# LSH attention and a token-mixing layer on one core: a new order of the same work, from a planner with other durations

## The chip, the cores and the metric

The kernel runs on one core of a Trainium2 chip. A time is the device time of one execution in microseconds (us). The kernel before was run three times; beside these there is one execution under the hardware profiler, with its own time and its trace.

The engines are named as in the profile: PE is TensorE (matmul), PEld its weight loads, DVE is VectorE, ACT is ScalarE, POOL is GpSimd, and SP is the queue from which all DMA is issued here.

## The reference

Four batches of eight heads, 768 positions, head size 64. Queries and keys are hashed to six sign bits by a random projection, a query sees only the keys of its own bucket, and the attention output, put together to 4 x 768 x 512, goes through a layer that mixes tokens with a phase:

```python
q_bits = (np.einsum('bhsd,dk->bhsk', q, proj) > 0)          # k alike; bits -> bucket
mask = q_bucket[:, :, :, None] == k_bucket[:, :, None, :]
scores = np.where(mask, scale * np.matmul(q, k.transpose(0, 1, 3, 2)), -1e9)
attn = np.exp(scores - np.max(scores, axis=-1, keepdims=True))
attn = attn / (np.sum(attn, axis=-1, keepdims=True) + 1e-09)
x = concat_heads(np.matmul(attn, v))                        # 4 x 768 x 512
theta = x @ w_theta
y = einsum('ts,bsd->btd', w_tok_r, x * np.cos(theta)) + einsum('ts,bsd->btd', w_tok_i, x * np.sin(theta))
u = x + y
out = u + np.maximum(u @ w_ch, 0.0)
```

## The kernel before

**Attention.** The unit is a *step*: one pair of heads, 128 rows of queries, all 768 keys; four batches of four pairs of six row tiles make 96 steps. In a trace or an order a step is written batch_pair_row, so 2_1_5 is the last row tile of the second pair of the third batch. A step runs through all engines:

- PE writes the scores of both heads, tile `st` (16 matmuls, two heads side by side). The bucket test is inside, as a rank-12 term of `rows` and `kb` with a large factor. Both halves of the PSUM pool "s" are taken by one step, so the scores of the next step start only as the exponentials of this one are done.
- DVE takes the maximum of each row of `st` (`mc`, L709) and makes shift and factor of it (L712, L715); ACT makes the exponential `pf` (L719), once for each head.
- ACT rounds `pf` to float16 (`pp`, L725), and POOL makes the rest as a second float16 (L731).
- SP issues a DMA transpose of both parts (`pt<-pp`, L735), one for each head.
- PE multiplies with the values (`po`, 18 matmuls for each head), which loads `pt` as weights. After three row tiles DVE divides (L767 to L779) and writes `x`.

`pb` are the matmuls of the hash bits, once for a pair of heads. Queries, keys, values and weights are split into a high and a low part on ACT, DVE and POOL.

**The layer.** When a batch's `x` is complete, PE transposes it (`pt_x`), multiplies with w_theta (`ps_th`, three matmuls in each part), ACT and DVE make cosine and sine (`z`, L895 and L896, which need another activation table than the exponential), PE multiplies over tokens (`py`, 36 matmuls for each of six row tiles), transposes (`pt_u`) and multiplies with w_ch (`ps_r`). The layer of one batch is put between the attention steps of the next; that of the last batch stands behind all attention.

**What sets the order.** Nothing is ordered by hand. The code builds a list of operations, each with a priority, one or more engines with a duration in ns, the operations it waits for and the buffers it takes (`op(...)`). `issue_all` plays that list through a model of the five engines: whenever an engine of the model is free, it takes the ready operation with the lowest priority number, and the instruction is emitted there. The order on each engine's queue is the order of these decisions; the chip then works each queue off in that order. The priority of an attention operation is its step number g plus an offset (`VM`, `PF`, `KA`, `KB`, `KT`, `KV`, `KN`); weights, values, queries and the layer have offsets of their own (`W0`, `WS`, `QK0`, `QK1`, `TH0`, `Y0`, `YS` and so on, those with `_0` and `_3` for the first and the last batch). `wl`, `wmul`, `qkl`, `sign`, `zl`, `zh` and `mag` name two engines, and the one that is free first gets them. Where PE in the model has nothing ready in the first 190 us of the model's time, a matmul on constants is emitted (`fill`), which keeps the clock up and computes nothing. Three tables bear on PE:

```python
AFTER = {"pv": 94, "vall": 70, "y": 17}
WIDE = {"st", "proj", "bits"}
if best is not None and o.name in WIDE:     # L241: another ready operation came first
if e != "PE" or o.name not in WIDE or AFTER.get(before, 0) < 50:   # L245
```

`pv` is `po` of the trace, `y` is `py`, `proj` is `ps_th` and `ps_r`, `bits` is `pb`. An operation in `WIDE` that would stand right behind a `pv` is put off for another ready one of about the same priority.

Of the kernel before, what the change touches and what calls it, by code (L numbers as in the profile page):

```python
# [31 lines left out]
def lsh_attention_moe_kernel(ctx: ExitStack, tc: tile.TileContext, qk, wt, v, consts, w_theta, w_ch, out):  # L32
# [59 lines left out]
    LAZY = dict.fromkeys(("wlow", "whigh", "wsign", "wabs", "wscale", "wmul", "wth", "wtl", "wh", "wl"), 200)  # L92
    WAKE = {"ACT": 45, "DVE": 37, "PE": 58, "POOL": 105, "SP": 40}
    AFTER = {"pv": 94, "vall": 70, "y": 17}
    WIDE = {"st", "proj", "bits"}
    SHARED = {"qkl", "p1", "p2", "zf", "zh", "zl", "mag", "wlow", "whigh", "wmul", "wl", "vv2", "wtl"}

    class Slot:
# [21 lines left out]
    def op(name, prio, alts, deps=(), slots=(), table=None):  # L120
        return Op(name, prio, alts, deps, slots, table)
# [472 lines left out]
    def prep_qk(b, hp, G, g):  # L594
        t = {}
# [34 lines left out]
        for lo, n_ in ((0, 512), (512, S - 512)):  # L630
            def signs(lo=lo, n_=n_):
                sm_ = Slot("m")
                u = {}

                def bits():
                    u["pb"] = bank(sm_, [P, 512], f"pb_{b}_{hp}_{lo}")
                    cols = slice(lo, lo + n_)
                    mm(u["pb"][:, :n_], pst["q"], t["hl"][:, 0, 0, cols], True, False)
                    mm(u["pb"][:, :n_], pst["k"], t["hl"][:, 0, 1, cols], False, False)
                    mm(u["pb"][:64, :n_], pst["q"][:, :64], t["hl"][:, 1, 0, cols], False, False)  # L640
                    mm(u["pb"][:64, :n_], pst["k"][:, :64], t["hl"][:, 1, 1, cols], False, True)

                def total():
                    if "sum" not in t:
                        t["rows"], t["kb"] = rowt[sr.idx], kbt[sr.idx]
                        t["sum"] = ap_.tile([56, S], F32, tag=sq.tag, bufs=1, name=f"sum_{b}_{hp}")
                    u["s"] = t["sum"][:, lo : lo + n_]
                    ACT.activation(u["s"], u["pb"][64:120, :n_], AF.Copy)

                def plus():  # L650
                    DVE.tensor_tensor(u["s"], u["pb"][:56, :n_], u["s"], ALU.subtract)

                def sign(eng):
                    return lambda: eng.tensor_scalar(t["rows"][:56, lo : lo + n_], u["s"], affs[:56, 0:1], affs[:56, 1:2], ALU.is_ge, ALU.mult)

                pr1 = G + at("QK1", b) + early
                b1 = op("bits", pr1, on("PE", 10 + 925 * n_ / 512, bits), hs + ls + [proj_ready], [sm_, sh])
                b1 = op("btot", pr1, on("ACT", 75 + 425 * n_ / 512, total), [b1], [sm_, sq, sr])
                b1 = op("bplus", pr1, on("DVE", 70 + 540 * n_ / 512, plus), [b1], [sm_, sq])
                fs.append(op("sign", pr1, {"DVE": (190 + 270 * n_ / 512, sign(DVE)), "POOL": (230 + 1940 * n_ / 512, sign(POOL))}, [b1], [sq, sr]))  # L660

            signs()
# [14 lines left out]
    def step(g, b, hp, i, t, vt, po):  # L677
# [15 lines left out]
                        l, r = (t["rows"][rows, ts(i, P)], t["kb"][rows, k0:k1]) if a == 2 else (hl[rows, a, 0, ts(i, P)], hl[rows, c, 1, k0:k1])  # L693
                        mm(st[j][:, k0:k1], l, r, n == 0, n == 3)

        a = op("st", g, on("PE", 1450, scores), t["ready"], ss + t["slots"])
        for j in range(2):
            def head(j=j):
                nonlocal a
# [47 lines left out]

                gj = g + DJ * j
                m = op("vmax", gj + VM, on("DVE", 865, vmax), [a], [ss[j], smc])
                m = op("factor", gj + VM, on("DVE", 70, factor), [m], [smc])  # L750
                m = op("shift", gj + VM, on("DVE", 70, shift), [m], [smc])
                e = op("pf", gj + PF, on("ACT", 680, pf), [m], [ss[j], smc, spf], table="exp")
                k1 = op("p1", gj + KA, pick(g, P1, {"ACT": (700, p1("ACT")), "DVE": (470, p1("DVE"))}), [e], [spf, spp])
                k2 = op("p2", gj + KB, pick(g, P2, {"DVE": (870, p2(DVE)), "POOL": (1650, p2(POOL))}), [k1], [spf, spp])
                d = op("turn", gj + KT, on("SP", [(1550, 515000)], turn), [k2], [spp, spt])
                po["done"] = op("pv", gj + KV, on("PE", 560, pv), [d] + po["wait"], [spt, po["slot"], vt["slot"], sx])
                po["wait"] = [po["done"]]

# [19 lines left out]
                rc = po["rc"].rearrange("p (i j) -> p i j", j=2)[:, :, j]  # L778
                DVE.scalar_tensor_tensor(dst, po["acc"][:, :, j, :D], vt["inv"], rc.unsqueeze(2).to_broadcast([P, HT, D]), ALU.mult, ALU.mult)  # L779

        r = op("total", g + KN, on("DVE", 90, total), [po["done"]], [po["slot"]])
        r = op("recip", g + KN, on("DVE", 70, recip), [r], [po["slot"]])
        n = op("norm", g + KN, on("DVE", 2 * 340, norm), [r], [po["slot"], sx])
        for k in range(lo, i + 1):
            xready[b][k].append(n)

# [184 lines left out]
    g = 0  # L971
# [19 lines left out]
BUFS = {'hl': 2, 'rows': 2, 'sum': 1, 'mc': 3, 'pf': 3, 'pp': 4, 'pt': 4, 'vb': 1, 'tmp': 3}  # L991
TAIL = ["m", "s"]
WIN = {"m": 3, "tmp": 3, "s": 2}
PF = -0.541
KA = 1.061
KB = 1.686
KT = 28.046
KV = 1.273
KN = 2.14
DJ = 0.23  # L1000
VM = -1.125
AB = -1.13
WTH = 23.785
WTS = -0.332
WC = 27.23
WCS = 0.768
P1 = [[0, 999, ['ACT']]]
P2 = [[0, 999, ['POOL']]]
GR = 2
GR1 = 0  # L1010
GROUPS = [[(0, 3), (3, 6)], [(0, 4), (4, 6)], [(0, 2), (2, 4), (4, 6)]]
TH0_3 = 1.836
TH1_3 = 0.0
Y0_3 = 15.352
YS_3 = 9.104
Y1_3 = 0.075
PV0_0 = -2.213
QK0_0 = -2.499
QK1_0 = -17.278
HOLD = 0.575  # L1020
FILL = 190000
TH0_0 = 0.433
TH1_0 = 0.727
Y0_0 = 12.725
Y1_0 = 2.214
YS_0 = 6.989
PEN = 1.489
AHEAD = 1.866
H0 = -9.299
PST = 19.565  # L1030
QKL = -13.487
QK0 = -4.416
QK1 = -4.289
PV0 = -2.541
LV0 = 1.74
W0 = 7.559
WS = 4.063
TH0 = 1.218
TH1 = 0.164
Y0 = 9.384  # L1040
YS = 6.051
Y1 = 2.833

EXTRA_INT = {"BUFS": [dict(hl=2, rows=2, sum=1, mc=3, pf=a, pp=b_, pt=c, vb=1, tmp=3) for a, b_, c in ((2, 3, 3), (3, 4, 4), (2, 4, 5), (3, 5, 3), (3, 3, 5), (2, 5, 4))]}
EXTRA_TUNE = ["DJ", "VM", "KT"]
# [51 lines left out]
```

## Time and profile before

| | |
|---|---|
| median of three runs | 810.58 us (808.44 to 811.03) |
| the profiled execution | 813.75 us, its span in the trace 811.9 us |
| PE busy | 771.1 us (95% of the span), 113.0 us of it filler |
| DVE, ACT, POOL busy | 564.8, 537.9 and 471.2 us (70, 66 and 58%) |
| matmuls | 7218, of which 463 are filler |
| DMA | 117.30 MB, 192 transposes |

The span is 1.85 us shorter than the time of the same execution, and that execution is 3.2 us (0.4%) above the median of the three others. The profile has for each group of instructions the busy time, the mean of one and the idle time just before it with its releaser. The busy time of PE is no measure of work done, since a matmul's end is modelled and follows its start by more than the next one needs; what one costs in a row of equal ones is the distance of their starts.

### The profile page before, as it was taken

The numbers are of one execution on the slowest core, as the hardware profiler recorded it, in microseconds if no ns is written. First come the engines' busy times: TensorE is split into PE (matmuls) and PEld (weight loads), VectorE is DVE, ScalarE is ACT, GpSimd is POOL, SyncE is SP. The second block draws the span as 40 slices with busy tenths as digits, with TensorE's granted clock in tenths as the row PEclk, the third lists the DMA queues.
The fourth block names the chain that finished last, engine by engine and source line by source line (L and its number), as shares of the span: only waits on it lengthen the run. The fifth ranks groups of instructions, "written<-read, shape, count | busy, mean of one in ns | idle before, by whom it ended". The sixth has DMA issues, their size and how long they took to land. (4 is left out here: it accounts for less than half of the span.)

```text
span 811.9 us, 18205 instructions
## 1 busy us (share of the span) xinstructions
PE 771.1 (95%) x7218; PEld 511.7 (63%) x7218; DVE 564.8 (70%) x1207; ACT 537.9 (66%) x712; POOL 471.2 (58%) x331
## 2 busy tenths in 40 slices
PE   9999998999997999999989999999999999999998
PEld 4556565667764466676756666667756776675456
DVE  6777887888878766676896566776876755557323
ACT  5767786677987675666996666666986665548101
POOL 4657665766765785756657576665476565533300
PEclk9999999999999999999999999999999999999999
DMA  6899999996575788978637998997339888850002
GB/s 221 181 184 214 168 230 226 172 213 137 89 161 115 152 169 155 191 160 170 111 73 146 161 180 158 185 182 165 59 74 191 158 132 156 148 113 0 1 1 78
DMA packets 322916, 117.30 MB, mean 144 GB/s; under 512 B 307920, under 2 KB 312016, under 8 KB 322832
## 3 DMA queue, kind: packets, MB, share of 16 engines
q1 hardware_dynamic: 322832, 116.15, 72.4%
q8 instruction: 56, 0.92, 0.5%
q14 instruction: 28, 0.23, 0.1%
HBM read 32.54 MB, written 6.29 MB: 48 GB/s over the span
## 5 line engine op out<-in xcount | busy, mean ns | idle before, releaser
L731 POOL TENSOR_TENSOR pp<-pf,pp 128x768 f16<-128x768 f32 x192 | 325.0, 1713 | 190.8 <-ACT pp L725 179.8
L719 ACT ACTIVATE pf<-st,mc 128x768 f32<-128x768 f32 x192 | 180.9, 988 | 119.1 <-DVE mc L715 73.7
L709 DVE TENSOR_REDUCE mc<-st 128x1 f32<-128x768 f32 x192 | 175.1, 950 | 84.0 <-PE st L83 83.6
L83 PE MATMUL py<-z,wtk 128*128 128x512 f16 x864 | 202.0, 379 | 1.0 <-DVE z L873 1.0
L83 PE MATMUL st<-hl 64*128 64x512 f32 (+1 forms) x1152 | 159.5, 355 | 7.2 <-ACT pf L719 6.7
L83 PEld LDWEIGHTS <-pt 128*128 128x128 f16 x3456 | 122.5, 98 | 54.8 <-DMA pt<-pp 27.3
L83 PE MATMUL po<-vv,pt 128*128 128x65 f16 (+1 forms) x3456 | 138.2, 195 | 16.9 <-DMA pt<-pp 14.8
L725 ACT ACTIVATE pp<-pf 128x768 f16<-128x768 f32 x192 | 152.7, 839 | 0.2
L83 PEld LDWEIGHTS st<-hl 64*128 64x128 f32 x1152 | 111.2, 186 | 57.3 <-ACT pf L719 29.2
L83 PEld LDWEIGHTS <-wtk 128*128 128x128 f16 x864 | 78.4, 98 | 85.5 <-issue 4.0
L83 PE MATMUL fill<-idle 128*128 128x512 f16 x463 | 113.0, 389 | 1.8 <-DVE ones L75 1.5
L918 POOL TENSOR_TENSOR z<-f,z 128x512 f16<-128x512 f32 x37 | 49.7, 1358 | 59.9 <-ACT z L912 40.6
L83 PE MATMUL st<-kb,rows 64*128 64x256 f32 (+1 forms) x384 | 81.0, 337 | 0.0
L83 PEld LDWEIGHTS <-idle 128*128 128x128 f16 x463 | 42.8, 100 | 49.4 <-issue 5.2
L83 PE MATMUL ps_r<-wch,h_u 128*128 128x512 f32 x192 | 64.8, 419 | 0.0
L83 PE MATMUL ps_th<-wth,h_x 128*128 128x512 f32 x192 | 62.7, 407 | 1.8 <-DVE l_x L838 1.4
L907 DVE SCALAR_TENSOR_TENSOR f<-x,zr,z 128x512 f32<-128x512 f32 x48 | 52.7, 1122 | 7.8 <-ACT z L895 5.1
L834 ACT ACTIVATE h_u<-pt_u 128x512 fp32r<-128x512 f32 x24 | 14.2, 594 | 58.1 <-PE pt_u L829 53.8
L83 PEld LDWEIGHTS st<-kb,rows 64*128 64x128 f32 x384 | 50.5, 187 | 3.2
L83 PE MATMUL ps_r<-wch,l_u 128*128 128x512 f32 x96 | 38.6, 402 | 3.3 <-DVE l_u L838 3.3
L83 PEld LDWEIGHTS ps_th<-wth,h_x 128*128 128x128 f32 x192 | 34.2, 189 | 10.2 <-DVE l_x L838 2.1
L83 PE MATMUL ps_th<-wth,l_x 128*128 128x512 f32 x96 | 38.2, 398 | 0.7 <-DVE l_x L838 0.7
(110 smaller groups left out, 875.6 us busy)
## 6 DMA issues: line engine op xcount, KB each, us to landing
nat<-in_qk_dram SPq DMA_DIRECT2D x32, 384.0 KB
wst<-in_wt_dram SPq DMA_DIRECT2D x12, 768.0 KB
vb<-in_v_dram SPq DMA_DIRECT2D x16, 384.0 KB
out_dram<-x SPq DMA_DIRECT2D x24, 256.0 KB
pt<-pp SPq DMA_TRANSPOSE x192
w_th<-in_moe_w_theta_dram SPq DMA_DIRECT2D x4, 512.0 KB
w_ch<-in_moe_w_ch_dram SPq DMA_DIRECT2D x8, 256.0 KB
kb<-rows SPq DMA_DIRECT2D x32, 36.0 KB
```

The lines of the kernel that those rows point to most:

```text
L83: PE.matmul(out_, l, r, start=start, stop=stop, skip_group_check=True)
L709: DVE.tensor_reduce(col(0), st[j], AX.X, ALU.max, negate=True)
L719: ACT.activation(u["pf"], st[j], AF.Exp, bias=col(2), scale=col(1))
L725: ACT.activation(u["pp"][:, 0], u["pf"], AF.Copy)
L731: return lambda: eng.tensor_tensor(u["pp"][:, 1], u["pf"], u["pp"][:, 0], ALU.subtract)
L834: ACT.activation(u["hi"], u["pt"], AF.Copy)
L907: DVE.scalar_tensor_tensor(u["f"], tl[b][:, tt], t["zr"][:, 2 * tt + r : 2 * tt + r + 1], t["zw"][r][:, tt], ALU.mult, ALU.mult)
L918: return lambda: eng.tensor_tensor(t["z"][r, 1][:, tt], u["f"], t["z"][r, 0][:, tt], ALU.subtract)
```

## The change

No instruction of the computation is added or taken away, no buffer count changes, and no size. What changes are the numbers from which the planner works: durations, the table `WIDE`, and all the offsets. The diff, with two lines for the table of offsets:

```diff
-    WIDE = {"st", "proj", "bits"}
+    WIDE = {"proj", "bits"}
...
-                b1 = op("bits", pr1, on("PE", 10 + 925 * n_ / 512, bits), hs + ls + [proj_ready], [sm_, sh])
+                b1 = op("bits", pr1, on("PE", -80 + 1080 * n_ / 512, bits), hs + ls + [proj_ready], [sm_, sh])
...
-        a = op("st", g, on("PE", 1450, scores), t["ready"], ss + t["slots"])
+        a = op("st", g, on("PE", 1600, scores), t["ready"], ss + t["slots"])
...
-                m = op("factor", gj + VM, on("DVE", 70, factor), [m], [smc])
-                m = op("shift", gj + VM, on("DVE", 70, shift), [m], [smc])
-                e = op("pf", gj + PF, on("ACT", 680, pf), [m], [ss[j], smc, spf], table="exp")
-                k1 = op("p1", gj + KA, pick(g, P1, {"ACT": (700, p1("ACT")), "DVE": (470, p1("DVE"))}), [e], [spf, spp])
-                k2 = op("p2", gj + KB, pick(g, P2, {"DVE": (870, p2(DVE)), "POOL": (1650, p2(POOL))}), [k1], [spf, spp])
-                d = op("turn", gj + KT, on("SP", [(1550, 515000)], turn), [k2], [spp, spt])
+                m = op("factor", gj + VM, on("DVE", 63, factor), [m], [smc])
+                m = op("shift", gj + VM, on("DVE", 121, shift), [m], [smc])
+                e = op("pf", gj + PF, on("ACT", 875, pf), [m], [ss[j], smc, spf], table="exp")
+                k1 = op("p1", gj + KA, pick(g, P1, {"ACT": (733, p1("ACT")), "DVE": (470, p1("DVE"))}), [e], [spf, spp])
+                k2 = op("p2", gj + KB, pick(g, P2, {"DVE": (870, p2(DVE)), "POOL": (1610, p2(POOL))}), [k1], [spf, spp])
+                d = op("turn", gj + KT, on("SP", [(1475, 720000)], turn), [k2], [spp, spt])
...
-        n = op("norm", g + KN, on("DVE", 2 * 340, norm), [r], [po["slot"], sx])
+        n = op("norm", g + KN, on("DVE", 655, norm), [r], [po["slot"], sx])
...
-KT = 28.046
-KV = 1.273
+KT = 55.822
+KV = 1.387
...
-W0 = 7.559
-WS = 4.063
+W0 = 27.21
+WS = 20.711
```

The second number of `turn` is a size from which the model works out how long a transpose holds the DMA engines: 515000 / 360 = 1430 ns before, 720000 / 360 = 2000 ns now.

What comes out is the same work in another order on every queue: 454 filler matmuls instead of 463; one more change to the sine table and back (in the layer of the third batch); and some operations that may run on two engines go to the other one, of which the most are six `zl` (L918) from POOL to DVE and three products of the token weights (L489, L490) from DVE to POOL. Three places follow.

PE, third batch, between the scores of step 2_1_5 and those of 2_2_0; `pt0` and `pt1` are the transposed exponentials of the two heads, and a row of `po` stands for 18. Before:

```order
L83 LDWEIGHTS pt0_2_1_3_6752
L83 MATMUL po_2_1_3_6825<-vv_2_1_5707,pt0_2_1_3_6752 128x65
...
L83 LDWEIGHTS pt1_2_1_3_6776
L83 MATMUL po_2_1_3_6825<-vv_2_1_5707,pt1_2_1_3_6776 128x65
...
L83 MATMUL ps_r1_1_6871<-wch0_3604,h_u1_1_6724 128x512
...
L83 MATMUL st0_2_2_0_6900<-hl_2_2_6243 128x512
```

and now:

```order
L83 LDWEIGHTS pt0_2_1_3_6739
L83 MATMUL po_2_1_3_6818<-vv_2_1_6176,pt0_2_1_3_6739 128x65
...
L83 MATMUL py_1_3_6574<-z1_1_5253,wtk0_95 128x512
...
L83 MATMUL ps_r1_1_6849<-wch0_3384,h_u1_1_6716 128x512
...
L83 LDWEIGHTS pt1_2_1_3_6768
L83 MATMUL po_2_1_3_6818<-vv_2_1_6176,pt1_2_1_3_6768 128x65
...
L83 MATMUL py_1_2_6358<-z1_1_5253,wtk0_95 128x512
...
L83 MATMUL st0_2_2_0_6896<-hl_2_2_6184 128x512
```

Between two steps' scores there stood 36 `po` in a row and then 12 `ps_r`; now the two heads' `po` stand apart, with three `py` and three `ps_r` behind the first and three `py` and six `ps_r` behind the second, and the other three `ps_r` stand between later `po`.

SP, first batch, from the transposes of step 0_0_3 to those of 0_0_4; `wst` are token weights, `w64_th` a part of w_theta, `vb` values. Before:

```order
L735 DMA_TRANSPOSE pt0_0_0_3_695<-pp0_0_0_3_636 128x12x128
L735 DMA_TRANSPOSE pt1_0_0_3_723<-pp1_0_0_3_643 128x12x128
L551 DMA vrow_105<-vam_0_2_750 1x128x1
L735 DMA_TRANSPOSE pt0_0_0_4_764<-pp0_0_0_4_725 128x12x128
L735 DMA_TRANSPOSE pt1_0_0_4_783<-pp1_0_0_4_747 128x12x128
```

and now:

```order
L735 DMA_TRANSPOSE pt0_0_0_3_689<-pp0_0_0_3_613 128x12x128
L544 DMA vb_0_2_713<-in_v_dram 128x2x384
L735 DMA_TRANSPOSE pt1_0_0_3_746<-pp1_0_0_3_635 128x12x128
L463 DMA wst_5_758<-in_wt_dram 128x1536
L403 DMA w64_th2_0_763<-in_moe_w_theta_dram 128x1024
L735 DMA_TRANSPOSE pt0_0_0_4_776<-pp0_0_0_4_742 128x12x128
```

Three loads that stood further off, one ahead of these rows and two behind them, are now issued between these transposes.

PE, the end of the attention, behind the last `po` of all; `x_3` is the fourth batch's `x`, and row tiles 3 to 5 of it are complete only after that `po`. Before:

```order
L83 MATMUL po_3_3_3_10608<-vv_3_3_9684,pt1_3_3_5_10745 128x65
...
L83 MATMUL ps_th3_1_10760<-wth0_93,h_x3_1_10735 128x512
...
L83 MATMUL ps_th3_2_10822<-wth0_93,h_x3_2_10784 128x512
...
L829 MATMUL pt_x3_3_10839<-ident_75,x_3_8744 128x128 x4
```

and now:

```order
L83 MATMUL po_3_3_3_10609<-vv_3_3_9741,pt1_3_3_5_10747 128x65
...
L83 MATMUL ps_th3_2_10793<-wth0_93,h_x3_2_10761 128x512
...
L829 MATMUL pt_x3_3_10831<-ident_75,x_3_8861 128x128 x4
```

Eighteen `ps_th` stood between the last `po` and the first transpose that needs its result; now six do, and the other twelve stand further ahead.

More of the change, by code (lines that the diff above doesn't have):

```diff
@@ L779, in norm @@
                 DVE.scalar_tensor_tensor(dst, po["acc"][:, :, j, :D], vt["inv"], rc.unsqueeze(2).to_broadcast([P, HT, D]), ALU.mult, ALU.mult)
-        r = op("total", g + KN, on("DVE", 90, total), [po["done"]], [po["slot"]])
-        r = op("recip", g + KN, on("DVE", 70, recip), [r], [po["slot"]])
-        n = op("norm", g + KN, on("DVE", 2 * 340, norm), [r], [po["slot"], sx])
+        r = op("total", g + KN, on("DVE", 72, total), [po["done"]], [po["slot"]])
+        r = op("recip", g + KN, on("DVE", 97, recip), [r], [po["slot"]])
+        n = op("norm", g + KN, on("DVE", 655, norm), [r], [po["slot"], sx])
         for k in range(lo, i + 1):
@@ L993 @@
 WIN = {"m": 3, "tmp": 3, "s": 2}
-PF = -0.541
-KA = 1.061
-KB = 1.686
-KT = 28.046
-KV = 1.273
[L999 to L1006, printed above, removed]
+PF = -0.076
+KA = 1.387
+KB = 3.495
+KT = 55.822
+KV = 1.387
+KN = 5.288
+DJ = 0.113
+VM = -1.039
+AB = -1.183
+WTH = 23.536
+WTS = -6.097
+WC = 26.894
+WCS = 4.189
 P1 = [[0, 999, ['ACT']]]
@@ L1011 @@
 GROUPS = [[(0, 3), (3, 6)], [(0, 4), (4, 6)], [(0, 2), (2, 4), (4, 6)]]
[L1012 to L1020, printed above, removed]
-FILL = 190000
[L1022 to L1035, printed above, removed]
-W0 = 7.559
-WS = 4.063
[L1038 to L1042, printed above, removed]
+TH0_3 = 0.242
+TH1_3 = 0.824
+Y0_3 = 18.235
+YS_3 = 10.019
+Y1_3 = -0.037
+PV0_0 = 1.145
+QK0_0 = 7.694
+QK1_0 = -66.396
+HOLD = 0.491
+FILL = 190000
+TH0_0 = 0.735
+TH1_0 = 0.785
+Y0_0 = 13.011
+Y1_0 = 1.853
+YS_0 = 6.291
+PEN = 3.68
+AHEAD = 1.986
+H0 = -38.347
+PST = 20.496
+QKL = -13.127
+QK0 = 1.039
+QK1 = -4.022
+PV0 = 2.295
+LV0 = 2.18
+W0 = 27.21
+WS = 20.711
+TH0 = 0.307
+TH1 = 0.291
+Y0 = 9.258
+YS = 5.867
+Y1 = 2.946
 EXTRA_INT = {"BUFS": [dict(hl=2, rows=2, sum=1, mc=3, pf=a, pp=b_, pt=c, vb=1, tmp=3) for a, b_, c in ((2, 3, 3), (3, 4, 4), (2, 4, 5), (3, 5, 3), (3, 3, 5), (2, 5, 4))]}
```

## The prediction

> **What bounds the kernel now.** I read the page first, then who PE waits for, then PE by stretches, and last single places in the timeline. Three lines of the page, and one of the view of the tile `fill`:
>
> ```profile
> span 811.9 us, 18205 instructions
> PE 771.1 (95%) x7218; PEld 511.7 (63%) x7218; DVE 564.8 (70%) x1207; ACT 537.9 (66%) x712; POOL 471.2 (58%) x331
> PE   9999998999997999999989999999999999999998
> L83 PE MATMUL fill<-idle x463: 376/379/634, 1.5 to 208.4; 128*128 128x512 f16 x155
> ```
>
> PE is busy throughout, but up to 208.4 us partly with filler: there, in the first batch, the steps go at the pace of the other engines, and filler and score matmuls share one queue. After that PE's own work and its waits set the end. All matmuls but filler stay, so the change can win only waits, filler and PE's changes from one kind of matmul to another. The waits, PE and weight loads apart:
>
> ```profile
> PE po L83 <- DMA pt<-pp: 14.8, 15, 2.5
> PE st L83 <- ACT pf L719: 6.7, 15, 1.3
> ...
> PE pb L83 <- DVE hl L621: 2.6, 1, 2.6
> PEld st L83 <- ACT pf L719: 29.2, 59, 1.6
> PEld L83 <- DMA pt<-pp: 27.3, 32, 2.7
> ```
>
> Columns are us in all, times, longest. Two waits matter: `po` for the transposed exponentials, and the next scores for the exponential that frees their PSUM. The longest stalls lie early in the second batch:
>
> ```profile
> 200.00:250.00 50.00, 44.81 (x435) 32.10 (x432) 41.77 (x75) 42.72 (x58) 37.16 (x26) 0.97 0.68 128
> 250.00:300.00 50.00, 45.10 (x429) 26.27 (x427) 37.57 (x86) 33.96 (x52) 33.51 (x27) 0.99 0.74 150
> 650.00:700.00 50.00, 49.52 (x550) 34.32 (x549) 27.15 (x69) 30.22 (x38) 28.51 (x20) 1.00 0.84 145
> ```
>
> After the stretch and its length stand the busy times of PE, PEld, DVE, ACT and POOL, then clock and DMA: 10 us of PE idle in the 100 us from 200 on, 0.5 us in the 50 us from 650 on.
>
> **The change part by part.** *Filler.* Nine fewer. One costs the distance of starts (the first line from the timeline, the others from the chain of waits):
>
> ```profile
> 34.85 3.40 PE L83 MATMUL fill<-idle 128*128 128x512 f16 x15
> 742.15 44.69 PE py L83 x207
> 733.78 8.37 PE ps_th L83 x36
> ```
>
> Fifteen in 3.40 us, the last lasting its 0.38: (3.40 - 0.38) / 14 = 0.216 us, so 9 x 0.216 = 1.9 us. If the other engines are the limit there, nothing is won: -1.9 to 0, I take **-1.9**, since PE shows nine tenths or more busy there. In the same way a `py` is 44.69 / 207 = 0.216 us and a projection matmul 8.37 / 36 = 0.233 us.
>
> *`po` behind its transposes.* What hides a transpose is PE work put between a step's scores and that step's `po`. Step 2_1_5:
>
> ```profile
> 465.14 1.17 PE L83 MATMUL st<-hl 64*128 64x512 f32 x6
> 466.95 1.56 PE L83 MATMUL po<-vv,pt 128*128 128x65 f16 x36
> 469.23 1.88 ACT L719 ACTIVATE pf<-st,mc 128x768 f32<-128x768 f32 x2 [0.71 <-DVE mc L715]
> 471.32 0.98 PE L83 MATMUL st<-hl 64*128 64x512 f32 x6
> 472.94 0.73 PE L83 MATMUL po<-vv,pt 128*128 128x65 f16 x18
> 473.50 0.81 PE L83 MATMUL py<-z,wtk 128*128 128x512 f16 x3
> 473.65 9.41 SPq L735 DMA_TRANSPOSE pt<-pp  x4
> 480.27 0.73 PE L83 MATMUL po<-vv,pt 128*128 128x65 f16 x18 [0.75 <-DMA pt<-pp]
> ```
>
> Its scores end at 466.95, its first `po` starts at 480.27, and PE waited 0.75 us. 18 `po` take 473.50 - 472.94 = 0.56 us, the 16 score matmuls 472.94 - 471.32 = 1.62. With these distances I added up, for each of the 192 transposes, the PE work that the two orders put there. The median goes from 13.2 to 13.9 us, the least from 7.2 to 8.4. For this step 11.7 becomes 12.4 us: three more `py`, 0.65 us, nearly the whole wait. Outside 205 to 290 us a mean wait of 14.8 / 15 = 1.0 us thus meets some 0.7 us more cover. There I took each wait, by the delay of the first `po`'s start, less the gain in its cover, and where cover shrinks by more than the transpose had to spare, the rest as a new wait: 16.4 us become 9.0, the longer one of each pair of heads counted, so -7.4 us.
>
> From 205 to 290 us it is otherwise. Step 1_1_1:
>
> ```profile
> 246.58 1.13 PE L83 MATMUL st<-hl 64*128 64x512 f32 x6
> 251.72 1.28 ACT L895 ACT_TABLE_LOAD   x1
> 256.73 1.88 ACT L719 ACTIVATE pf<-st,mc 128x768 f32<-128x768 f32 x2
> 264.43 3.66 SPq L735 DMA_TRANSPOSE pt<-pp  x2
> 268.81 0.73 PE L83 MATMUL po<-vv,pt 128*128 128x65 f16 x18 [1.91 <-DMA pt<-pp]
> ```
>
> 22 us from scores to `po`, since its exponential stood behind sine and cosine and their tables. In the new order that step has 0.7 us less cover, the next, 1_1_2, has 12.7 us instead of 19.4. If the transposes land as late behind their scores as they did, new waits there (the longer one of each pair of heads, less the old ones) come to 12 us. But the order on ACT and POOL was made anew with PE's, so I charge a third: +4.0. Together **-3.4**, between -14.8 (all of today's PE waits gone) and +4.6 (-7.4 and the full 12).
>
> *Scores behind the exponential.* Above, scores end at 466.95 and the second exponential at 469.23 + 1.88 = 471.11: 4.2 us later. Of the 95 gaps between steps' scores, 34 held less than 4.2 us of PE work and 16.0 us too little in all; now 9, with 7.3. Half of the 6.7 us goes: **-3.5**, between -6.7 and 0.
>
> *The clock.* Five stretches of 4 us, from the same view as above:
>
> ```profile
> 41.00:45.00 4.00, 2.70 (x31) 1.88 (x32) 3.85 (x11) 2.53 (x4) 1.30 (x2) 0.68 1.01 210
> 73.00:77.00 4.00, 4.00 (x24) 1.70 (x21) 1.36 (x8) 3.65 (x5) 2.96 (x3) 0.57 1.28 212
> 247.00:251.00 4.00, 3.09 (x34) 2.52 (x31) 4.00 (x5) 2.06 (x4) 3.29 (x2) 0.57 0.91 199
> 370.00:374.00 4.00, 4.00 (x35) 3.16 (x32) 3.13 (x7) 1.92 (x3) 4.00 (x3) 0.57 0.51 97
> 561.00:565.00 4.00, 4.00 (x37) 3.62 (x36) 3.46 (x5) 1.56 (x3) 3.69 (x3) 0.57 0.29 53
> ```
>
> Each closing costs 4 x 0.43 = 1.7 us of PE and follows a cluster of stalls. With fewer stalls I take one fewer of the last three: **-1.7**; all three gone would be -5.1, two more +3.4. The Trainium skill, "TensorE: Matmul & The Clock Gate", section "HAM oscillation — how this bites in real kernels", sums its rule up as no PE-idle gap over about 3.4 us. No wait of PE here is over 2.6 us and the clock still halved, so the trace does not bear that out as a safe bound; by it the term would be 0 and the sum 1.7 us higher.
>
> *Kinds of matmul.* Behind `po` a projection part starts slower:
>
> ```profile
> 493.57 0.71 PE L83 MATMUL ps_r<-wch,h_u 128*128 128x512 f32 x2
> 494.12 0.39 PE L83 MATMUL ps_r<-wch,l_u 128*128 128x512 f32 x1
> 494.34 0.63 PE L83 MATMUL ps_r<-wch,h_u 128*128 128x512 f32 x2
> 494.81 0.40 PE L83 MATMUL ps_r<-wch,l_u 128*128 128x512 f32 x1
> ```
>
> 0.55 us to the third matmul, then 0.47: 0.08 us. Such places fall from 37 to 20: -1.4 at most, 0 if the step behind `py` costs the same; **-0.7**. Scores right behind `po`, which the new table allows, rise from 8 to 14; at the same 0.08 us that is **+0.5**, bounds 0 and +0.5.
>
> *The end of the attention.*
>
> ```profile
> 726.01 0.73 PE L83 MATMUL po<-vv,pt 128*128 128x65 f16 x18
> 727.20 0.74 DVE L779 SCALAR_TENSOR_TENSOR x<-po,vinv,rc 128x192 f32<-128x192 f32 x2
> 730.86 1.03 PE L829 MATMUL pt_x<-ident,x 128*128 128x128 f32 x8
> ```
>
> `x` is done 1.2 us after the last `po` (727.94 against 726.74). Eighteen `ps_th` hid that; six, 1.4 us, still do, and with that cover gone it costs 1.2. The `po` of 3_3_2 to 3_3_4 come 0.1 to 2.0 us earlier behind their scores, where some had little to spare: **+2.0**, between 0 and +3.
>
> *ACT, DVE, POOL, SP.* One more pair of table loads is 2 x 1.28 = 2.6 us of ACT. Mostly hidden under `py`, since scores there lie further apart; **+0.5**, between 0 and 2.6. The Trainium skill, "ScalarE: Activation LUTs", section "What ACT_TABLE_LOAD costs", gives 2.66 us a switch with its drain; here the sine starts at 253.01, right behind 251.72 + 1.28, so no drain shows; by the page the upper bound would be 5.3 us and the sum would go up to 1 us. Six `zl` leave POOL for DVE, which has 8 us and more free in each 50 us above; 0. The loads now ahead of 0_0_4's transposes are met by 1.5 and 3.0 us more cover of that step: 0, and up to +2 if not.
>
> Sum: -1.9 - 3.4 - 3.5 - 1.7 - 0.7 + 0.5 + 2.0 + 0.5 = -8.2. The profiled execution took 813.75 us, 1.85 over its span and 3.2 over the median of the runs shown. From it: 805.6; from the median 810.6: 802.4. The change is timed by runs like the latter, so **802 us**.
>
> **The rivals.** *Late transposes in the second batch (slower).* The full 12 us fall due: 8.0 more than charged, 810.4; the clock term turns from -1.7 to +3.4 as more stalls cluster, 815.5: about **815**. It decides from about 6 us of new waits. For it: the 22 us above, and that 14 of the 20 transposes there lose cover. Against: the new duration for the exponential is 875 ns, close to 1.88 / 2 = 0.94 (680 before), so the new order places what follows closer to when it comes.
>
> *Waits only move (no change).* The weight loads' 29.2 us in 59 behind the exponential say that many waits lie one under the other: a `po` that comes sooner lets the next scores reach a PSUM that isn't free. Of 8.2 us some 7 return: 810.6 - 1.2, **809**. Against: gaps too short for that fall from 34 to 9.
>
> *All of it at once (faster still).* `po` waits and score waits go, 14.8 + 6.7, and 1.9 of filler, less 3 for the end and tables: -20.4, **790**. For it: cover grows in most places from 290 us on; against: steps differ by more than 0.7 us.
>
> **How the numbers follow.** Forecast 0.52, late transposes 0.20, waits move 0.20, all at once 0.08. The forecast's own range is 796 to 808; with the others, 789 to 816. A measurement of this kernel tells 0.3% (2.4 us) from no change: faster is below 808.1, slower above 813.0. Faster: 0.08 and 0.50 of the forecast, 0.04 of waits that move: 0.62. Same: 0.02 + 0.13 + 0.02 of the late transposes: 0.17. Slower: 0.18 + 0.03: 0.21.
>
> **What would show it.** PE's wait for the transposes below 12 us, that for the exponential below 4; filler 454 times, ending about 2 us earlier; at most four halvings of the clock behind the first; PE above 45.5 us busy in each 50 us from 200 to 300. I am wrong if `po` waits 20 us or more, or if PE's idle time is the same in another place.

## The result: 2.5% faster, 13 us more than forecast

| | before | now |
|---|---|---|
| median of four runs | 810.35 us (808.44 to 811.03) | 789.25 us (787.72 to 792.47) |
| ratio to before, 95% interval | | 0.9749 (0.9712 to 0.9785) |
| the profiled execution | 813.75 us, span 811.9 | 790.16 us, span 788.4 |
| filler matmuls | 463 | 454 |
| the clock halved, in windows of 3.41 us | 5 | 2 |

The forecast was 802 us, 8 us faster; it became 21 us from median to median and 23.6 us between the profiled executions. The time lies at the lower edge of the range, 789, and beside the rival "all of it at once", 790, to which I had given 0.08; that it lies so close to the rival is chance, as the last part shows.

The page of the changed kernel, its lines that answer to those of before, and then the view of the tile `fill` (shortest, median and longest in ns, first and last start):

```profile
span 788.4 us, 18212 instructions
PE 760.2 (96%) x7209; PEld 505.1 (64%) x7209; DVE 559.8 (71%) x1215; ACT 535.7 (68%) x712; POOL 468.0 (59%) x325
PE   8999899999889999999999999999999999989997
```

```profile
L83 PE MATMUL fill<-idle x454: 376/379/634, 1.5 to 187.5; 128*128 128x512 f16 x152
```

The row of tenths shows 9 (90% or more) from the thirteenth slice on but for two slices, at the end of the attention and of the layer. PE's busy time fell by 10.9 us and the span by 23.5, so more than half of the gain is time in which PE had stood still. Who PE waits for, in the view of waits:

```profile
PE st L83 <- ACT pf L719: 7.1, 19, 0.9
PE po L83 <- DMA pt<-pp: 3.4, 6, 1.4
PE fill L83 <- DVE sum L651: 2.1, 1, 2.1
...
PEld st L83 <- ACT pf L719: 31.8, 68, 1.2
PEld L83 <- DMA pt<-pp: 10.4, 18, 1.9
```

The waits of `po` for its transposes went from 14.8 us in 15 to 3.4 in 6, and those of its weight loads from 27.3 to 10.4. The waits of scores for the exponential did not shrink at all: 6.7 in 15 became 7.1 in 19. PE by stretches:

```profile
200.00:250.00 50.00, 45.20 (x402) 31.66 (x402) 42.10 (x79) 45.03 (x59) 29.21 (x18) 0.97 0.67 127
250.00:300.00 50.00, 49.24 (x510) 30.72 (x508) 40.14 (x96) 38.12 (x61) 40.43 (x31) 1.00 0.88 171
600.00:650.00 50.00, 49.99 (x557) 34.76 (x554) 30.45 (x77) 32.41 (x42) 31.13 (x23) 1.00 0.90 157
```

From 250 to 300 us PE now works 49.24 us, where it had worked 45.10 and done 429 matmuls against 510. From 200 to 250 it stays at 45. The granted clock fell in two places (and, as before, in the last 2 us, when PE has ended):

```profile
14.00:18.00 4.00, 3.16 (x8) 1.16 (x8) 3.86 (x7) 2.78 (x6) 3.39 (x2) 0.63 0.31 100
212.00:217.00 5.00, 4.62 (x36) 3.75 (x37) 4.71 (x7) 4.80 (x8) 4.75 (x4) 0.66 0.13 37
```

The trace records the clock in windows of 3.41 us; I count one at half speed as half of it, 1.7 us. Before there were five (17.1 us), now two (6.8 us). The distances of starts bear the price out: inside these windows they are 8.4 us longer before, and 3.0 us now, than between the same pairs of matmuls elsewhere.

**Where 23.5 us of span went.** I took three quantities from both traces. Filler: 9 x 0.216 = 1.9 us. Clock: (17.1 - 6.8) / 2 = 5.1 us. `po` behind its transposes: for each step the delay of the first `po`'s start behind what PE did before it, the longer one of the two heads, 18.5 us before and 5.3 now, so 13.2 us. That leaves 23.5 - 20.2 = 3.3 us, which the rows don't give to one cause. In the views of waits, PE's waits other than those of scores and `po` changed places, but their sum did not move: 12.5 us before, 12.7 now. Filler's rose from 1.8 to 5.8 us, and that of `pb` (2.6 us) is gone; two lines of them, the first of before, the others of now:

```profile
PE ps_r L83 <- DVE l_u L838: 3.3, 3, 1.4
```

```profile
PE fill L83 <- DVE x L779: 2.0, 1, 2.0
PE ps_r L83 <- DVE l_u L838: 0.3, 1, 0.3
```

By batches of the attention:

| | batch 1 | batch 2 | batch 3 | batch 4 |
|---|---|---|---|---|
| `po` waits before, us | 7.3 | 4.7 | 4.6 | 2.0 |
| as my count had them for the new order | 3.5 | 14.8 | 2.5 | 2.1 |
| measured | 3.7 | 1.1 | 0.5 | 0.0 |

The count was right for the first batch, near for the third, and wrong by 13.7 us for the second, just where I had expected the new order to be short of cover. By the times at which the same steps' scores start, the gain stands at 1.7 us at step 1_0_0, is gone to a loss of 1.4 at 1_1_0, then 3.5 us at 1_1_3, 9.1 at 1_2_0, 16.6 at 2_1_0 and 23.8 at 3_1_0. These starts compare only as far as the same work stands ahead of them: by the distances of starts the new order has 0.2 us less of it ahead of 1_0_0, 1.9 less at 1_1_0 and 3.8 less at 3_1_0.

So the sum of 20.2 us does not close by place. Ahead of 1_0_0 the waits of `po` fell by 3.6 us, the clock by 1.7 and two of the nine fillers are gone (0.4), 5.7 us, and the gain is 1.7: 4.0 us are lost there, as much as filler's waits rose. Behind it the three came to 14.5 us, and 21.8 were won. The 3.3 us left over are the difference of 7.3 and 4.0.

Step 1_1_1 itself, whose 22 us from scores to `po` the prediction showed; its timeline after the change:

```profile
251.75 0.49 PE L83 MATMUL st<-hl 64*128 64x512 f32 x1
254.60 5.35 PE L83 MATMUL py<-z,wtk 128*128 128x512 f16 x24
257.25 1.87 ACT L719 ACTIVATE pf<-st,mc 128x768 f32<-128x768 f32 x2 [1.19 <-DVE mc L715]
262.66 3.31 SPq L735 DMA_TRANSPOSE pt<-pp  x2
268.17 0.73 PE L83 MATMUL po<-vv,pt 128*128 128x65 f16 x18
```

The exponential starts 5.5 us behind the first score matmul (257.25 - 251.75), where it had been 10.2 (256.73 - 246.58): the tables of the sine and back are now loaded at 242.79 and 247.67 us, ahead of its scores, where they had stood between scores and exponential (251.72 and 255.44). The transposes are issued 10.9 us behind instead of 17.9, and `po` starts without a wait, 16.4 us behind instead of 22.2. Measured from the end of its scores, the two transposes of 1_1_1 land 12.4 and 14.2 us later instead of 19.8 and 21.4, those of 1_1_2 after 11.8 and 13.6 instead of 20.3 and 22.1, while those of 1_1_0 went from 11.8 and 13.6 to 16.4 and 18.4: the sine and cosine now delay another step, which has the cover. Over all 192 transposes the median landing stayed at 13.0 us behind the scores, while the median time to spare between landing and `po` rose from 1.1 to 1.5 us, and the transposes with under 0.5 us to spare fell from 53 to 33.

### The profile page after: what moved, and what is told of

It reads as the page before. It is cut to its first block, busy times and chain, and to the rows that moved or that the text cites. A ratio compares the mean times of both kernels' runs of the same rounds, so it can differ in the third digit from the quotient of the medians.

```text
span 788.4 us, 18212 instructions
## 1 busy us (share of the span) xinstructions
PE 760.2 (96%) x7209; PEld 505.1 (64%) x7209; DVE 559.8 (71%) x1215; ACT 535.7 (68%) x712; POOL 468.0 (59%) x325
## 4 chain that ended last, share of the span: by engine, by line
PE 65%; DVE 12%; ACT 9%; DMA 8%; issue 3%; SPq 1%; POOL 0%; ACTq 0%; DVEq 0%; POOLq 0%
PE py L83 21%; PE st L83 15%; PE po L83 9%; PE ps_r L83 7%; PE fill L83 5%; PE ps_th L83 5%; DVE mc L709 5%; DMA pt<-pp 4%; ACT pf L719 3%; ACT pp L725 2%; PE pb L83 2%; DMA nat<-in_qk_dram 1%; PE pt_u L829 1%; DVE wst L472 1%; ACT n L870 1%
## 5 line engine op out<-in xcount | busy, mean ns | idle before, releaser
L731 POOL TENSOR_TENSOR pp<-pf,pp 128x768 f16<-128x768 f32 x192 | 328.7, 1730 | 193.9 <-ACT pp L725 174.9
L83 PE MATMUL st<-hl 64*128 64x512 f32 (+1 forms) x1152 | 156.7, 355 | 7.3 <-ACT pf L719 7.1
L83 PEld LDWEIGHTS <-pt 128*128 128x128 f16 x3456 | 120.9, 97 | 41.7 <-issue 11.9
L83 PEld LDWEIGHTS st<-hl 64*128 64x128 f32 x1152 | 106.4, 185 | 57.1 <-ACT pf L719 31.8
L83 PE MATMUL fill<-idle 128*128 128x512 f16 x454 | 110.9, 388 | 5.9 <-DVE sum L651 2.1
L83 PE MATMUL st<-kb,rows 64*128 64x256 f32 (+1 forms) x384 | 77.0, 335 | 0.0
L918 POOL TENSOR_TENSOR z<-f,z 128x512 f16<-128x512 f32 x31 | 41.3, 1342 | 53.6 <-ACT z L912 31.4
L83 PE MATMUL ps_r<-wch,h_u 128*128 128x512 f32 x192 | 67.5, 433 | 0.1
L834 ACT ACTIVATE h_u<-pt_u 128x512 fp32r<-128x512 f32 x24 | 14.2, 596 | 57.8 <-PE pt_u L829 46.3
L907 DVE SCALAR_TENSOR_TENSOR f<-x,zr,z 128x512 f32<-128x512 f32 x48 | 45.4, 967 | 8.3 <-ACT z L895 6.0
L83 PEld LDWEIGHTS st<-kb,rows 64*128 64x128 f32 x384 | 46.9, 186 | 4.0
L83 PEld LDWEIGHTS ps_r<-wch,h_u 128*128 128x128 f32 x192 | 35.1, 189 | 9.6 <-ACT h_u L834 0.3
L83 PEld LDWEIGHTS ps_th<-wth,h_x 128*128 128x128 f32 x192 | 34.4, 189 | 10.4 <-DVE l_x L838 2.2
```

Of the source, the lines that this page charges most:

```text
L83: PE.matmul(out_, l, r, start=start, stop=stop, skip_group_check=True)
L731: return lambda: eng.tensor_tensor(u["pp"][:, 1], u["pf"], u["pp"][:, 0], ALU.subtract)
L834: ACT.activation(u["hi"], u["pt"], AF.Copy)
L907: DVE.scalar_tensor_tensor(u["f"], tl[b][:, tt], t["zr"][:, 2 * tt + r : 2 * tt + r + 1], t["zw"][r][:, tt], ALU.mult, ALU.mult)
L918: return lambda: eng.tensor_tensor(t["z"][r, 1][:, tt], u["f"], t["z"][r, 0][:, tt], ALU.subtract)
```

## The experiments

The theories, as the expectations name them. **A**: what decides is the cover of the transposes and exponentials on PE's queue, with the halvings of the clock that follow from stalls. **B**: the truer durations are the gain, **C**: the offsets are, and **D**: `WIDE` does nothing. **E**: the transposes are hidden anyway and SP has time to spare. **F**: the gain comes from elsewhere. **G**: each set of numbers is fitted as a whole, so any move away from it costs (G1 for the kernel before as well, G2 only for now, the kernel before lying anywhere among its neighbours).

All runs in one table. Ratios are to the kernel before as it was timed beside each, medians with their interval; the other columns are from one profiled execution each. "Rest" is what is left of the difference in span to the kernel before (811.9) once filler (0.216 us each), half of the halved time and the `po` waits, summed as above, are taken off.

| kernel | ratio (95% interval) | span | filler | halved, us | `po` waits, us | rest |
|---|---|---|---|---|---|---|
| before | 1 | 811.9 | 463 | 17.1 | 18.5 | 0 |
| now | 0.9749 (0.9712 to 0.9785) | 788.4 | 454 | 6.8 | 5.3 | -3.3 |
| before, new durations | 1.0279 (1.0233 to 1.0324) | 832.8 | 480 | 37.5 | 17.4 | 8.1 |
| before, new offsets | 1.0280 (1.0244 to 1.0317) | 831.6 | 492 | 20.5 | 21.3 | 8.9 |
| before, new `WIDE` | 1.0282 (1.0250 to 1.0314) | 834.4 | 471 | 37.5 | 22.4 | 6.7 |
| now, old `WIDE` | 1.0003 (0.9976 to 1.0029) | 807.4 | 454 | 17.1 | 11.5 | 4.4 |
| now, old durations of `turn` | 1.0523 (1.0490 to 1.0557) | 851.0 | 471 | 58.0 | 26.4 | 9.0 |
| before, late transposes | 1.0159 (1.0129 to 1.0188) | 823.0 | 463 | 20.5 | 28.7 | -0.8 |
| now, late transposes | 0.9866 (0.9849 to 0.9882) | 798.8 | 454 | 3.4 | 17.6 | -3.4 |
| now, `WC` moved | 0.9872 (0.9852 to 0.9893) | 799.6 | 454 | 10.2 | 14.9 | -3.3 |
| now, `Y0` moved | 1.0048 (1.0020 to 1.0076) | 815.9 | 454 | 30.7 | 9.0 | 8.6 |
| before, `PEN` moved | 1.0043 (1.0019 to 1.0067) | 818.4 | 463 | 30.7 | 26.1 | -7.9 |
| before, `Y0` moved | 1.0053 (1.0023 to 1.0083) | 816.8 | 463 | 17.1 | 20.1 | 3.3 |
| now, filler everywhere | 0.9817 (0.9782 to 0.9851) | 797.6 | 559 | 6.8 | 4.5 | -15.9 |

### One part of the change at a time

The durations alone, in the kernel before with its own offsets and `WIDE`:

```diff
-        a = op("st", g, on("PE", 1450, scores), t["ready"], ss + t["slots"])
+        a = op("st", g, on("PE", 1600, scores), t["ready"], ss + t["slots"])
...
-                e = op("pf", gj + PF, on("ACT", 680, pf), [m], [ss[j], smc, spf], table="exp")
+                e = op("pf", gj + PF, on("ACT", 875, pf), [m], [ss[j], smc, spf], table="exp")
...
-                d = op("turn", gj + KT, on("SP", [(1550, 515000)], turn), [k2], [spp, spt])
+                d = op("turn", gj + KT, on("SP", [(1475, 720000)], turn), [k2], [spp, spt])
```

> The kernel before with the new durations alone; offsets and the table WIDE stay old. Counted from its order with the distances of starts of before's trace: 480 filler, median cover between scores and po 13.4 us (13.2 before, 13.9 after), but its lowest tenth 9.5 us (11.3 before, 11.9 after), and gaps between scores too short by 23.1 us in all (16.0 before, 7.3 after). Theory A (the time goes with PE's waits for transposes and for the exponential, and with the clock halvings that follow them, so what counts is cover): 808 to 822 us, no better than before. Rival B (the planner's truer durations are the gain, whatever the offsets): 788 to 800 us.

The offsets alone:

```diff
-KT = 28.046
-KV = 1.273
+KT = 55.822
+KV = 1.387
...
-W0 = 7.559
-WS = 4.063
+W0 = 27.21
+WS = 20.711
```

> The kernel before with the new offsets alone; durations and WIDE stay old. 492 filler, median cover 13.3 us, lowest tenth 10.8 us, short gaps 18.9 us. Theory A (cover decides): 806 to 820 us. Rival C (the gain is where the offsets put weights and layer, early in each batch): 788 to 800 us.

And `WIDE` alone:

```diff
-    WIDE = {"st", "proj", "bits"}
+    WIDE = {"proj", "bits"}
```

> The kernel before with scores taken out of the table WIDE and nothing else. The order differs from step 0_1_3 on, in a third of its pieces; 471 filler, median cover 12.9 us, lowest tenth 10.2 us. If that table is what made 790 of 811 us in the run with the old WIDE: 790 to 800 us here. Theory A by its count of cover: 812 to 820 us. Theory G1: 815 us or more.

Measured: 834.4, 834.3 and 836.3 us. Each part by itself costs 2.8%; the three together win 2.5%. The view of waits and the clock of the kernel with the new durations alone:

```profile
PE po L83 <- DMA pt<-pp: 16.3, 12, 3.5
PE st L83 <- ACT pf L719: 11.9, 23, 2.2
```

```profile
core 0: 832.8 us, clock 0.977
```

The kernel with the new offsets alone, and then the one with the new `WIDE` alone:

```profile
PE po L83 <- DMA pt<-pp: 19.0, 24, 2.6
PE st L83 <- ACT pf L719: 8.1, 16, 1.0
```

```profile
PE po L83 <- DMA pt<-pp: 20.2, 20, 2.7
PE st L83 <- ACT pf L719: 8.6, 13, 1.7
PE pt_x L829 <- DVE z L873: 4.2, 1, 4.2
```

All three still wait for their transposes as the kernel before does; with the new durations the scores wait almost twice as long, and eleven windows of the clock are halved instead of five. B and C fall: neither the truer durations nor the offsets carry the gain. So does the guess that the new `WIDE` alone makes 790 to 800 us. A had the sign, but put the first two at 806 to 822 us and the third at 812 to 820, and was 12, 14 and 16 us short.

### One part taken back

```diff
-    WIDE = {"proj", "bits"}
+    WIDE = {"st", "proj", "bits"}
```

> The kernel after with the old table WIDE, so that scores are again put off when they would stand right behind po. 454 filler as after, median cover 13.9 us as after, lowest tenth 10.8 us (11.9 after), short gaps 17.1 us (7.3 after). Theory A: some 5 to 12 us of waits come back, 794 to 801 us. Rival D (which matmul stands behind which doesn't matter, nor do short gaps): 788 to 791 us, as after.

```diff
-                d = op("turn", gj + KT, on("SP", [(1475, 720000)], turn), [k2], [spp, spt])
+                d = op("turn", gj + KT, on("SP", [(1550, 515000)], turn), [k2], [spp, spt])
```

> The kernel after with the old figures for the DMA transpose alone (1430 instead of 2000 ns on the DMA engines in the planner's model). 471 filler, median cover 13.1 us, lowest tenth 10.3 us, short gaps 18.2 us: po is planned 0.8 us closer behind its scores again. Theory A: PE's wait for transposes back to 12 to 20 us and the time to 803 to 814 us. Rival B (any of the truer durations, the exponential's above all): 790 to 797 us.

Measured: 811.0 us, the time of before, with the old `WIDE` (A: 794 to 801), and 854.7 with the old durations of the transpose. The waits of the first:

```profile
PE st L83 <- ACT pf L719: 14.8, 27, 1.5
PE po L83 <- DMA pt<-pp: 9.8, 10, 2.0
PE ps_th L83 <- DVE mc L715: 4.8, 2, 3.5
```

Up to the scores of 1_1_2 its order is that of now. By the starts of the same steps' scores it lies 0.5 us ahead of now at 1_2_0, 4.3 behind at 2_0_0, 10.9 at 2_1_0 and 16.1 at 3_3_5. The next scores wait twice as long for their PSUM, 14.8 us against 7.1; of the 19.0 us of span against now these are 7.7, the `po` waits 6.2 and the clock 5.1. D falls, though the edit moves more than the scores, and their place was not tested by itself. The second, its waits and its clock:

```profile
PE po L83 <- DMA pt<-pp: 25.8, 25, 2.5
PE st L83 <- ACT pf L719: 6.4, 11, 1.5
```

```profile
core 0: 851.0 us, clock 0.965
```

Seventeen windows are halved, 58.0 us. Of the 62.6 us of span against now, the clock is (58.0 - 6.8) / 2 = 25.6, the `po` waits 21.1, filler 17 x 0.216 = 3.7, and 12 remain. One pair of numbers of the model, 1550 instead of 1475 ns on SP and 1430 instead of 2000 ns of DMA for a transpose, moves the time by more than the whole change did; which of the two does it was not tested. A expected 803 to 814 us here: the waits that it names are there, but their size was not foreseen.

### What a late transpose costs, with the order held

The order stays as it is in both kernels, and ahead of each of the 192 transposes SP issues one more DMA, four bytes into a scratch tile that nobody reads:

```diff
+                    dma(late[0:1, late_n[0] : late_n[0] + 1], consts[0:1, 0:1])
+                    late_n[0] += 1
```

In the kernel before:

> The kernel before with one 4-byte DMA more ahead of each of the 192 transposes (into a scratch tile nobody reads), which the planner doesn't know: every queue keeps its order. Each such DMA holds SP for some 0.35 to 0.6 us, so the first head's transpose goes out 0.4 to 0.5 us later, the second's 0.8 to 1.0. From before's trace, what each transpose had to spare before its po: 50 to 58 steps would wait longer, by 25 to 34 us in all if nothing absorbs it. Theory A (PE's waits for transposes are what the order is about): 825 to 845 us. Rival E (SP has slack, transposes are hidden anyway): 809 to 813 us.

In the changed kernel:

> The kernel after with the same 192 extra DMAs, again with every queue's order unchanged. From after's trace 28 to 34 steps would wait longer, by 11 to 16 us in all. Theory A: 797 to 806 us, and about half of the loss that the same edit brings to before. Rival E: 788 to 792 us. Rival F (both orders stand equally close to their transposes, and the gain is elsewhere): the same loss as before, 805 us or more.

The tile `late` and the waits, first of the kernel before with this edit, then of the changed one with it, where the edit shifts the lines by two:

```profile
L737 SPq DMA_DIRECT2D late<-in_consts_dram x192: 265/440/1207, 25.9 to 732.5; - x192
```

```profile
PE po L83 <- DMA pt<-pp: 23.6, 25, 2.7
```

```profile
L737 SPq DMA_DIRECT2D late<-in_consts_dram x192: 248/438/1060, 27.1 to 709.5; - x192
```

```profile
PE po L83 <- DMA pt<-pp: 15.8, 19, 1.6
PE st L83 <- ACT pf L721: 8.9, 20, 1.4
```

Medians rose by 14.0 us (810.8 to 824.8, where A had 825 to 845) and by 10.9 (789.25, measured at another time, to 800.1, within A's 797 to 806). Here the accounts close. Before: `po` waits 10.2 us more, halved clock 3.4 us more, so 10.2 + 1.7 = 11.9 us expected, and the span rose by 11.1. Now: `po` waits 12.3 us more, halved clock 3.4 us less, 12.3 - 1.7 = 10.6 us, and the span rose by 10.4. So a wait of `po` for its transpose is paid one to one, and E falls: of 192 x 0.44 = 84 us of added issue time on SP, some 11 us come out on PE. A had expected the changed kernel to lose half of what the one before loses. It loses about three quarters by the medians, with intervals that don't tell it from the same loss, and by the waits of `po` rather more (12.3 us against 10.2). So F's premise, that both orders stand equally close to their transposes, is not refuted by this; its second half, that the gain lies elsewhere, does not fit the waits of `po` that fell by 13.2 us.

### Small moves of one offset

```diff
-WC = 26.894
+WC = 27.0
```

> The kernel after with one offset moved slightly (w_ch, 26.894 to 27.0). The order is the same up to step 1_1_0 and differs from there in about an eighth of its pieces; counted cover is nearly that of after (median 13.9, lowest tenth 11.6, short gaps 8.7 us against 7.3). Theory A (cover decides): 788 to 796 us. Rival G (after's order is a lucky point, and any change of it costs as much as the old WIDE did): 800 to 815 us.

```diff
-Y0 = 9.258
+Y0 = 9.4
```

> The kernel after with another offset moved slightly (the token products, 9.258 to 9.4). The order is the same up to step 2_0_3 and differs from there in about a seventh of its pieces; counted cover is worse: lowest tenth 10.4 us (11.9 in after), short gaps 21.2 us (7.3). Theory A: 797 to 808 us, worse than with the offset of w_ch moved. Rival G: 800 to 815 us, the same as there.

`WC` is the offset at which the weights w_ch are prepared, `Y0` that of `py` in the first batch's layer. Measured: 801.0 us and 815.0 us, 1.3 and 3.1% above now by the ratios. The waits of the two, `WC` first:

```profile
PE po L83 <- DMA pt<-pp: 14.2, 18, 2.9
PE st L83 <- ACT pf L719: 8.6, 16, 1.5
```

```profile
PE st L83 <- ACT pf L719: 17.6, 28, 2.4
PE po L83 <- DMA pt<-pp: 7.2, 11, 1.4
PE po L83 <- DVE z L873: 5.3, 1, 5.3
```

With `WC` moved, the order is that of now up to step 1_1_0. Cover, counted as in the prediction, has the same median, 13.9 us, and gaps too short for the exponential hold 8.7 us against 7.3; by the count the kernel should have taken the time of now. It took 11 us more, of which `po` waits are 9.6, and by the starts of scores 9.5 are lost between 1_1_0 and 1_3_0. So counted cover alone doesn't say what an order takes. With `Y0` moved the order is the same to step 2_0_3; some 14 us are lost between 3_0_0 and 3_1_0 and 6 behind the last scores, scores wait 17.6 us, and nine windows are halved. The 5.3 us in the last line are no wait for a transpose: those of that step, 3_0_0, had landed by 554.0 us, and its `po` starts at 563.67. It takes a buffer of the PSUM pool "m", as the `ps_th` that z reads does, and starts as z ends. The count of cover has no term for that.

The same kind of move in the kernel before, `PEN` 1.489 to 1.45 and `Y0` 9.384 to 9.5:

> The kernel before with one offset moved slightly (the limit PEN, 1.489 to 1.45). The order is the same up to step 1_0_3 and differs from there in a tenth of its pieces. Theory G1 (each table is fitted, so that any move of one number costs some per cent, in before as in after): 816 to 830 us. Theory G2 (before lies anywhere among its neighbours, and only after is a rare good order): 803 to 816 us, on either side of before.

> The kernel before with another offset moved slightly (the token products, 9.384 to 9.5). The order is the same up to step 2_3_1 and differs from there in a twentieth of its pieces. Theory G1: 813 to 825 us. Theory G2: 805 to 815 us, on either side of before.

Measured: 816.0 and 816.2 us, ratios 1.0043 and 1.0053, both intervals above 1. The waits of the first and then of the second:

```profile
PE po L83 <- DMA pt<-pp: 23.6, 22, 3.3
```

```profile
PE po L83 <- DMA pt<-pp: 17.2, 16, 2.3
```

Every neighbour of either kernel by such a move is slower than it, by 0.4 to 0.5% at the old numbers and by 1.3 to 3.1% at the new ones; where durations or `WIDE` were taken back it was 2.6 to 8%. At the new numbers that is G's sign. At the old ones the two moves cost 3.5 and 3.7 us against 812.5 us measured beside them; 816.0 lies on the border between G1's range and G2's, 816.2 within G1's and 1.2 us above G2's. That leans to G1 and doesn't exclude G2; two small moves on each side are too few for a distribution.

### Filler wherever the model is idle

```diff
-FILL = 190000
+FILL = 900000
```

> The kernel after with filler allowed to the end, wherever the planner sees PE idle: 559 filler instead of 454. If the clock halvings behind PE's waits matter by themselves, filler in the waits keeps the clock up and the time falls by up to 2 x 1.7 us, 785 to 789 us. If the planner's idle places are not where PE waits on the chip, 105 x 0.216 = 22.7 us of filler come on top of the work: 795 to 812 us.

Measured: ratio 0.9817, 0.7% above that of now, with intervals that touch (0.9785 and 0.9782); the span of the profiled execution is 9.2 us longer. Its page and waits:

```profile
PE 775.2 (97%) x7314; PEld 512.2 (64%) x7314; DVE 564.7 (71%) x1215; ACT 535.9 (67%) x712; POOL 468.7 (59%) x325
```

```profile
PE st L83 <- ACT pf L719: 4.2, 10, 0.9
...
PE po L83 <- DMA pt<-pp: 3.3, 5, 1.1
```

105 more fillers are 22.7 us of work. Some 13 us of them fell into time in which PE stood still anyway, 9 were paid, and the halved windows remained two. The 785 to 789 us of the first guess were missed. Where the model sees an idle PE, the chip's PE has often something to do.

## Why the prediction was right or wrong

**What bounds the kernel: right.** The gain is in PE's queue: filler, clock and the waits of `po` come to 20.2 of 23.5 us, though not place by place.

**Filler: the count right, its worth not shown.** Nine fewer, at most -1.9 us. The 1.7 us won at step 1_0_0 do not measure it, since only two of the nine are missing ahead of that step and seven behind it. In the run with 105 more of them 9 of their 22.7 us were paid. What I offered as its sign was none: the last filler starts 20.9 us earlier (187.5 against 208.4), not 2.

**`po` behind its transposes: the step that failed.** Forecast -3.4, measured -13.2. The step is "If the transposes land as late behind their scores as they did". With landings held where they had been, the stretch from 205 to 290 us came to 12 us of new waits, of which I charged a third, +4.0. The landings had moved with the order: at 1_1_1 and 1_1_2, where cover shrank, the transposes came 7 to 8.5 us sooner behind their scores. Cover and landing moved together, and in the planner's code they must: its `pv` waits for its `turn`. Which of the new numbers brought the landings forward no run separates; what the trace shows is that the sine's tables left that place. I let the planner's new order reduce the charge to a third, and it should have taken it away. Outside that stretch I counted 16.4 us down to 9.0. Measured, all 96 steps wait 5.3 us, of which no more than 1.1 are in the second batch; so 16.4 became 4.2 to 5.3, and -7.4 should have been -11 to -12.

**Scores behind the exponential: wrong.** Forecast -3.5, measured +0.4 (6.7 to 7.1 us on PE) and +2.6 on the weight loads. Short gaps fell as counted, and the waits stayed. The count took 4.2 us from scores to exponential for every step, which is the median in both traces (4.2 and 4.3); but of the eight steps of now whose scores wait longest, six stand behind an exponential that ended 6.2 to 8.4 us behind its scores. Taking back `WIDE`, with which these waits are 14.8 us, points to the place of the scores as well, but moves more than that.

**The clock: right direction, too small.** Forecast -1.7, measured -5.1: all three of the later halvings that I named are gone, and so are the two in the first batch; two new ones came, neither where an old one was. That the bound of -5.1 is the measured value is chance, since it stood for the three later ones alone. The Trainium skill, "TensorE: Matmul & The Clock Gate", section "HAM oscillation — how this bites in real kernels", puts the rule as keeping idle gaps of PE under about 3.4 us. Now, too, the trace doesn't bear it out as a bound: the longest wait of PE is 2.1 us, and two windows were halved. By the rule that term would have been 0.

**The end of the attention: wrong.** Forecast +2.0, and nothing of it shows. The chain of waits at the end, before and then now:

```profile
726.74 4.30 PE ps_th L83 x18
...
733.12 0.66 PE pt_x L829 x4
733.78 8.37 PE ps_th L83 x36
```

```profile
705.06 0.57 PE po L83 x18
705.63 1.49 PE ps_th L83 x6
...
707.14 0.69 ACT n L870
...
709.21 0.66 PE pt_x L829 x4
709.86 8.42 PE ps_th L83 x36
```

From the end of the last `po` to the 36 `ps_th` it takes 733.78 - 726.74 = 7.04 us before and 709.86 - 705.63 = 4.23 now: 2.8 us less, just what the twelve `ps_th` cost that now stand ahead (12 x 0.233). PE stands idle 1.2 us before the last four transposes in both. So the six `ps_th` cover `x` as the eighteen did. Nor did the `po` of the last steps wait: those of the fourth batch went from 2.0 us to none.

**Kinds of matmul, tables, POOL to DVE: not told apart.** They came to +0.3 us in the sum. What is left of the difference once the +0.4 of the scores is taken out of the 3.3 us, -3.7 us, holds them and the end of the attention; none was measured by itself, so some 4 us of the gain stay without a cause.

**The rivals.** Late transposes in the second batch, 815 us: refuted at its place, since the `po` waits of that batch fell from 4.7 to 1.1 us. Waits only move: right for the scores, wrong for the sum. All of it at once: the time was met by luck, since the score waits stayed, and the clock, which it left out, gave 5.1 us. I had no row for how landings move and took the old ones.

**What I had said would show it.** Wait for transposes below 12 us: 3.4. For the exponential below 4: 7.1, missed. At most four halvings: two. PE above 45.5 us in each 50 from 200 to 300: 45.20 and 49.24, so missed in the first and far above in the second.

**What stays open.** Why neighbouring orders take 1 to 3% more is shown only as far as the columns of the table go: halved clock, `po` waits, and a rest that scatters by 8 or 9 us either way with no single cause. Of the nine kernels for which A gave a range, one came out within it, the changed one with late transposes; late transposes in the kernel before missed it by 0.2 us, and all seven with another order were slower than its range, by 5 to 41 us. So the counted cover did not give the size for any other order. That the numbers of both kernels were chosen by timing many orders would fit with it; it is not shown here. No run beat the change.

## What to carry to other kernels

Where one planner sets the order on all engines, count the cover of a wait together with the time at which what is waited for will come in the new order: a chain's length taken from the old trace holds only where its own queue has not moved. Then time the order: here the count came out too slow for the changed kernel and too fast for seven other orders. Costs, offsets and tables of such a planner work as one set: here each of three parts alone cost 2.8%, and together they won 2.5%, so neither a part's merit nor the truth of its durations tells its effect. A wait of the bounding engine was paid about one to one while the order was held (11.9 us against 11.1, and 10.6 against 10.4), and stalls that fall into one window of the clock cost once more.

## What the hardware did that was not expected

The halved clock could move the time more than the waits for transposes did: 17.1 us at half speed before, 6.8 now, and 58.0 with the durations of `turn` taken back, where it makes 25.6 of 62.6 us and the `po` waits 21.1. It came though no wait of PE in the view of waits was over 2.6 us before and 2.1 us now. What went with it was PE's idle time in the window before. Cut at the borders of the clock's records, the 14 profiled executions hold 3212 windows of 3.41 us at full clock. PE was idle, by the ends that the trace gives, 1.85 us or more in 47 of them, and the window behind each of these was halved; it was idle less than 1.25 us in 3077, and behind none of these was it halved; of the 88 between, 29 were followed by a halved one. And a DMA of four bytes held SP for 0.44 us in the median, about a quarter of a transpose's 1.65; 192 of them, 84 us of SP's time, brought 11 us of span.
